# Two ways to place the second batch's turned keys and queries in a fused attention and SwiGLU kernel: by VectorE and by DMA

## The chip, the cores and the metric

The kernel runs on one core of one Trainium2 chip. The metric is the device time of one execution in microseconds; lower is better. The time before is the median of three runs, and a further execution was profiled.

## The reference

Block-sparse attention over q, k, v of shape (4, 8, 768, 64) (batch, heads, sequence, head size), then a gated feed-forward layer over the 3072 tokens with 512 features each.

```python
scores = scale * np.matmul(q, k.transpose(0, 1, 3, 2))      # scale = 1 / sqrt(64)
mask = np.abs(blk_i - blk_j) <= 1                           # blocks of 32 positions
mask = mask | (blk_i == 0) | (blk_j == 0) | (blk_i == 23) | (blk_j == 23)
# and three sampled key blocks for each query block
scores = np.where(mask, scores, -1e9)
attn = softmax(scores)
x = np.matmul(attn, v)                                      # heads side by side: (3072, 512)
xn = x / np.sqrt(np.mean(x * x, axis=-1, keepdims=True) + 1e-06) * rms_g
g = xn @ w_gate                                             # (512, 1536)
out = (g * sigmoid(g) * (xn @ w_val)) @ w_out               # (1536, 512), float32
```

## The kernel before

**Groups and heads.** The work goes in nine groups of rows (called gi). Batch 0 has three groups (gi 0 to 2) of two 128-row tiles; batches 1 to 3 have two groups each (gi 3 to 8) of three tiles. `FIRST` is 3, the first group of batch 1. A group goes through its eight heads in order. For a head, `scores` makes the scores in parts (two in batch 0, three after): PE multiplies `KT` by `QT` into the PSUM tile `st` (L325), and ACT takes the exponential into `ex` (L328). The mask is not a step of its own: 24 more rows of `KT` and `QT` carry it into the product. One head later `late_pv` multiplies `ex` by the values (L336, tile `op`), and DVE divides by the row sums (`rz` L345, `stage` L346).

**The feed-forward pieces.** When a group's attention is done, its rows are scaled (`squares` L370, `rstd` on POOL at L378, `xs`), turned (`tx`, `xg`) and put into a list `fill` of small pieces, which the next group's heads take up one by one at each call of `position()`, four in a head. A gate piece is four matmuls into `gp` (L437) and a tanh on ACT into `th` (L441). A val piece is four matmuls into `vp` (L448) and two DVE instructions: `u` (L452, reads `th` and `gp`) and `hps` (L454, reads `u` and `vp`). A down piece multiplies `hps` by the output weights (`yp` L465); after every fourth of them ACT writes `yo` and SP stores it (L472). `gp`, `vp` and `yp` share three PSUM buffers in turn, so that a `vp` waits until the `u` of the gate before the last has read its `gp`, and a `gp` until a `hps` has read its `vp`.

**Keys and queries of batches 1 to 3.** They come by POOL's DMA queue into `kbf` and `qbf`, a pair of heads at a time (pairs 0 to 3; for batch 1, pairs 0 and 1 early in group 1, pairs 2 and 3 late in group 2). `turn` turns one of them by a DMA transpose on SP's queue (L299) into a `turned` tile, of which there are four buffers in turn. `place` copies the two halves (w = 0 and 1) of a turned tile, 64 partitions of 768 elements each, to partitions 0 to 63 of `KT` or `QT`: for pairs 0 and 1 of batch 1 by DVE (L308), for all others by DMA on SP's queue (L310). Every instruction in a queue waits for those before it: DVE's copies stand among its `u` and `hps`, SP's placings among its turns and stores.

**The order written by hand.** For batch 1 the dictionary `early` says when each step is issued. Its keys count heads from the start of group 2: 0 to 7 are group 2, 8 to 11 the first heads of group 3. A step is a letter and a number: `t` turns, `p` places, and the number is twice the pair, plus 1 for queries. So t0 turns the keys of pair 0 and p3 places the queries of pair 1. All of a head's steps come at its end, in `turns`, after the head's scores, its `late_pv` and its pieces. t4 to t7 use the buffers of t0 to t3 again, so each has to wait until that one is placed. From head 4 of group 3 on, `turns` also turns batch 2 (and later batch 3), a head each, and places the oldest turned tile a head later (`ready`). Heads 2p and 2p + 1 of group 3 are the first that need pair p of batch 1.

Of the kernel before, what the change touches and what calls it, by code (L numbers as in the profile page):

```python
# [18 lines left out]
def kernel(  # L19
# [17 lines left out]
    nc = tc.nc  # L37
    P = 128
    B, H, S, D = q.shape
# [14 lines left out]
    FIRST = NC // 2  # L54
# [39 lines left out]
    def load_qk(b, pr):  # L94
        load_one(b, pr, kbf)
        load_one(b, pr, qbf)

    def load_v(b, pr):
        t = ld.tile([P, 2, NC, D], FP32, name="vraw", tag="vraw" if b else "vraw0",
                    bufs=2 if b else 4)  # L100
        nc.gpsimd.dma_start(  # L101
            out=t, in_=v[b, 2 * pr:2 * pr + 2].rearrange("e (p c) d -> p e c d", p=P))
        vraw[(b, pr)] = t
# [4 lines left out]
    def load_gv(lo, hi):  # L108

        for t, src in ((wg, moe_w_gate), (wv, moe_w_val)):  # L110
            nc.gpsimd.dma_start(
                out=t[:, :, lo * P:hi * P],
                in_=src.rearrange("(c p) f -> p c f", p=P)[:, :, lo * P:hi * P])
# [17 lines left out]
    for h in range(2):  # L131
        for which, src in ((0, k), (1, q)):
# [3 lines left out]
                out=f32[:, 0:cols],  # L136
                in_=src[0, h].rearrange("(p c) d -> p (c d)", p=P)[:, 0:cols])
# [5 lines left out]
    def halves(which, b):  # L143

        if which == 0:
            return KT[b % 2][0:D].rearrange("p h (w c s) -> p h w c s", w=2, s=P)
        return QT[b % 2][0:D].rearrange("p h (c w s) -> p h w c s", w=2, s=P)
# [69 lines left out]
    def mask_keys(lo, hi):  # L217
# [11 lines left out]
                      in_=kind.unsqueeze(1).to_broadcast([NB, H - 4, S]))  # L229
    samp = samp_i[:].rearrange("p (a r w) -> p a r w", r=NRND, w=2)[:, :, :, 0]  # L230
    for r in range(NRND):
        nc.vector.scalar_tensor_tensor(
            out=bm[0:NB, :], in0=samp[0:NB, :, r], scalar=kc[0:NB, :], in1=bm[0:NB, :],
            op0=ALU.is_equal, op1=ALU.max)

    def mask_queries(third):

        c_lo = 2 * third
        cuts = [0] + [(32 * m - c_lo + NC - 1) // NC for m in (1, 2)] + [16]
        for m in range(3):  # L240
            lo, hi = cuts[m], cuts[m + 1]
            nc.vector.tensor_scalar(
                out=qmask.rearrange("p (c i r) -> p c i r", c=NC, r=16)[
                    :, c_lo:c_lo + 2, :, lo:hi],
                in0=bm[0:NB, :].rearrange("p (i m) -> p i m", m=3)[:, :, m].unsqueeze(
                    1).unsqueeze(3).to_broadcast([NB, 2, 8, hi - lo]),
                scalar1=-MASKV, scalar2=MASKV, op0=ALU.mult, op1=ALU.add)

    def spread_queries(third, lo):

        c_lo, c_hi = 2 * third * P, 2 * (third + 1) * P
        nc.sync.dma_start(
            out=QT[0][D:KR, lo:H, c_lo:c_hi],
            in_=qmask[:, c_lo:c_hi].unsqueeze(1).to_broadcast([NB, H - lo, c_hi - c_lo]))
# [38 lines left out]
    turned = {}  # L293
# [9 lines left out]
    def place(b, pr, which):  # L303
        t = turned.pop((b, pr, which))
        view = halves(which, b)[:, 2 * pr:2 * pr + 2]
        for w in range(2):
            if b == 1 and pr < 2:
                nc.vector.tensor_copy(out=view[:, :, w], in_=t[w * D:(w + 1) * D])  # L308
            else:
                nc.sync.dma_start(out=view[:, :, w], in_=t[w * D:(w + 1) * D])  # L310

    def ex_tile(n):
        t = work.tile([P, NC * TGM], BF16, name="ex", tag="ex", bufs=3)
# [2 lines left out]
    def scores(grp, h, part, ex):  # L316

        b, c0, n = grp
        tg = n * P
        nj = 2 if n == HC else 3  # L320
        st = ps_s.tile([P, 1024], FP32, name="st", tag="st")
        at = st.rearrange("p (j t) -> p j t", t=512 if n == HC else tg)
        for e in range(nj):
            jt = nj * part + e
            nc.tensor.matmul(  # L325
                out=at[:, e, 0:tg], lhsT=KT[b % 2][0:KR, h, jt * P:(jt + 1) * P],
                rhs=QT[b % 2][0:KR, h, c0 * P:c0 * P + tg], start=True, stop=True)
        nc.scalar.activation(  # L328
            out=ex[:, nj * part:nj * (part + 1), :], in_=at[:, 0:nj, 0:tg], func=AF.Exp,
            scale=SCALE)  # L330
# [212 lines left out]
    def side_work(gi, h):  # L543

        if gi == 1:
            if h == 0:
                load_gv(3 * NF // 4, NF)
                nc.gpsimd.dma_start(out=wo, in_=moe_w_out.rearrange("(c p) f -> p c f", p=P))
            if h == 1:
                load_qk(1, 0)  # L550
                load_qk(1, 1)
                load_v(1, 0)
                load_v(1, 1)
                held_q.append(qbf[(1, 1)])
            if h == 3:
                mask_queries(2)
                spread_queries(2, 1)
        if gi == FIRST and h == 1:
            nc.gpsimd.dma_start(
                out=gain, in_=moe_rms_g.unsqueeze(0).to_broadcast([P, DM]))  # L560
        if gi == 2 and h == 1:
            for T, m in ((KT, kind), (QT, qmask)):
                nc.gpsimd.dma_start(out=T[1][D:KR, :, :],
                                    in_=m.unsqueeze(1).to_broadcast([NB, H, S]))
        if gi == 2 and h == 2:
            load_one(1, 2, qbf, held_q.pop())
            load_one(1, 2, kbf)
            load_qk(1, 3)
# [9 lines left out]
    def casts(gi, b, g, h):  # L578
# [14 lines left out]
        if b + 1 < B:  # L593
            load_v(b + 1, 2 * g + n)
            load_qk(b + 1, 2 * g + n)

    def turns(gi, b, g, h):


        if gi in (FIRST - 1, FIRST):  # L600
            for step in early.get((gi - FIRST + 1) * H + h, ""):
                pair, which = divmod(int(step[1:]), 2)
                (turn if step[0] == "t" else place)(1, pair, which)
        ready = next(iter(turned), None) if gi > FIRST or (gi == FIRST and h > 3) else None
        if 0 < b < B - 1 and h >= 4:
            turn(b + 1, 2 * g + (h - 4) // 2, h % 2)
        if ready is not None:
            place(*ready)

    early = {0: ("t0", "t1", "t2", "t3"), 5: ("p0",), 6: ("p1", "t4", "t5"),  # L610
             7: ("p2", "t6"), 8: ("p3", "t7", "p4"), 9: ("p5",), 10: ("p6",), 11: ("p7",)}

    TX = 2

# [90 lines left out]
    for gi, grp in enumerate(groups):  # L705
        if gi == 0:
            continue
        b, c0, n = grp
        g = c0 // n
        parts = 3 if n == HC else 2  # L710
        cur = begin(grp)
        for h in range(H):
            ex = ex_tile(n)
            thin = gi == 1 and h < TX
            scores(grp, h, 0, ex)
            if h == 0 and groups[gi - 1][2] == HC:
                squares(waiting[0][0], 2, 0, (H - 1) * D)
            if h == 1 and ending is not None:
                rms_scale(ending, 1)
            if h == TX and ending is not None:  # L720
                transpose_x(ending, 0)
                if gi == 1:
                    transpose_x(ending, 1)
                    enter(ending, NPOS + 4)
                    ending = None
            if thin and h > 0:
                keep_busy(1, 512)
            position()
            if gi == 1 and h == 0:
                late_pv()  # L730
                last = late_pv()
            scores(grp, h, 1, ex)
            side_work(gi, h)
            position()
            if h == TX and ending is not None:
                transpose_x(ending, 2)
            if h == 1 and ending is not None:
                rms_scale(ending, 2)
            if thin:
                keep_busy(1, 512)  # L740
            if gi > 1 or h > 0:
                last = late_pv()
            if last is not None:
                ending = last
            position()
            if parts == 3:
                scores(grp, h, 2, ex)
            position()
            while later:
                later.pop(0)()  # L750
            if h == TX and ending is not None:
                transpose_x(ending, 1)
                enter(ending, NPOS - 2 if gi == len(groups) - 1 else NPOS)
                ending = None
            turn_first(gi, h)
            casts(gi, b, g, h)
            turns(gi, b, g, h)
            if gi == FIRST and h == 5:
                nc.vector.tensor_scalar(out=gain, in0=gain, scalar1=float(DM) ** 0.5,
                                        scalar2=None, op0=ALU.mult)  # L760
            if h == 0 and ending is not None:
                rms_scale(ending, 0)
            if h == H - 1 and n == HC:
                squares(cur, 1, 0, (H - 1) * D)
            waiting.append((cur, h, ex))
# [50 lines left out]
```

## Time and profile before

| | |
|---|---|
| median of 3 runs | 310.85 us (310.80 to 310.89) |
| profiled execution | 311.14 us |
| its span, from the first to the last instruction | 309.4 us |
| PE busy | 298.9 us (97% of the span) |
| DVE busy | 205.9 us (67%) |
| ACT busy | 204.5 us (66%) |
| mean granted TensorE clock | 0.998 |

Times in the views are microseconds from the start of the span; "x4" in a timeline means that four instructions of the same kind were merged into the row, and brackets give the idle time before it and what ended that. PE is TensorE's matmuls, DVE is VectorE, SPq is the queue that issues SyncE's DMAs: a DMA's row there is the time of its issue, and it lands later. Group 2 ends and group 3 begins at about 66 us: its first scores (384 columns wide instead of 256) are the row "66.09 0.49 PE L325 MATMUL st<-QT,KT 88*128 88x384 bf16 x2". With three such rows to a head, head 1 begins at 69.50, head 2 at 73.63, head 4 at 81.68 and head 6 at 89.11.

### The profile page before, as it was taken

The page shows a single profiled execution, that of the slowest core. Times are in us where ns is not written, and L with a number is a line of the kernel's source. Part 1 is how long each engine was busy: PE and PEld are TensorE (multiplying, and loading weights), DVE is VectorE, ACT ScalarE, POOL GpSimd, SP SyncE. Part 2 cuts the span into 40 slices and gives each one's busy share as a digit, 9 for nine tenths or more (in the row PEclk, how much of TensorE's full clock was granted, in tenths as well). Part 3 has the DMA queues.
Part 4 walks back from the last instruction along what each step waited for, and adds up shares of the span by engine and source line. Part 5 has one row for each costly group of instructions (what it writes and reads, how often), then busy time and mean ns, then how long its engine had stood idle before and what let it go on. Part 6 is the DMA issues. An engine that isn't in the chain of part 4 may idle for free.

```text
span 309.4 us, 7249 instructions
## 1 busy us (share of the span) xinstructions
PE 298.9 (97%) x2844; PEld 198.6 (64%) x2864; DVE 205.9 (67%) x568; ACT 204.5 (66%) x330; POOL 55.7 (18%) x81
## 2 busy tenths in 40 slices
PE   7898999999999999999999999999999999999995
PEld 5677886975777566656666566655666566655653
DVE  7888884896668667773768457682767546675850
ACT  4896775775878677657776676676767666733321
POOL 9947120132220212012200122010000100010000
PEclk9999999999999999999999999999999999999999
DMA  7999999899997478506683378714000130002002
GB/s 143 289 205 201 209 245 121 149 189 173 211 170 140 112 155 163 126 20 189 114 157 87 87 170 129 152 30 141 13 2 0 49 106 2 0 18 87 2 0 102
DMA packets 59645, 36.04 MB, mean 117 GB/s; under 512 B 37472, under 2 KB 55204, under 8 KB 59612
## 3 DMA queue, kind: packets, MB, share of 16 engines
q0 software_dynamic: 17120, 17.90, 32.5%
q1 hardware_dynamic: 42456, 17.68, 26.1%
q8 instruction: 22, 0.36, 0.5%
q14 instruction: 11, 0.09, 0.1%
q10 hardware_dynamic: 36, 0.01, 0.1%
HBM read 28.59 MB, written 6.29 MB: 113 GB/s over the span
## 4 chain that ended last, share of the span: by engine, by line
PE 86%; DVE 7%; DMA 2%; issue 1%; SPq 1%; ACT 1%; POOL 0%; DVEq 0%
PE yp L465 20%; PE gp L437 19%; PE vp L448 19%; PE st L325 18%; PE op L336 10%; DMA QT<-turned 2%; SPq L310 1%; DVE junk L370 1%; DVE KT L291 1%; PE tx L419 1%; DVE QT L291 1%; DVE stage L363 1%; DVE hps L454 1%; ACT ex L328 1%; DVE u L452 0%
## 5 line engine op out<-in xcount | busy, mean ns | idle before, releaser
L328 ACT ACTIVATE ex<-st 128x768 bf16<-128x768 f32 x186 | 149.8, 812 | 54.9 <-PE st L325 53.0
L325 PE MATMUL st<-QT,KT 88*128 88x384 bf16 (+1 forms) x432 | 93.8, 308 | 3.4 <-DVE QT L291 1.9
L437 PE MATMUL gp<-xg,wg 128*128 128x384 bf16 (+1 forms) x432 | 80.8, 307 | 0.0
L448 PE MATMUL vp<-xg,wv 128*128 128x384 bf16 (+1 forms) x432 | 80.2, 307 | 0.6 <-DVE u L452 0.6
L452 DVE SCALAR_TENSOR_TENSOR u<-th,gp 128x384 bf16<-128x384 bf16 (+1 forms) x108 | 54.8, 507 | 38.4 <-ACT th L441 36.8
L465 PE MATMUL yp<-wo,hps 128*128 128x512 bf16 (+1 forms) x283 | 71.9, 369 | 0.9
L441 ACT ACTIVATE th<-gp 128x384 bf16<-128x384 f32 (+1 forms) x108 | 48.9, 453 | 27.9 <-PE gp L437 27.7
L454 DVE TENSOR_TENSOR hps<-u,vp 128x384 bf16<-128x384 bf16 (+1 forms) x108 | 55.1, 510 | 11.6 <-DVE u L452 0.5
L325 PEld LDWEIGHTS <-KT 88*128 88x128 bf16 x432 | 41.2, 98 | 28.5 <-DVE QT L291 2.8
L448 PEld LDWEIGHTS <-wv 128*128 128x128 bf16 x432 | 40.6, 97 | 21.5 <-issue 1.0
L437 PEld LDWEIGHTS <-wg 128*128 128x128 bf16 x432 | 40.1, 97 | 20.5 <-issue 0.3
L336 PEld LDWEIGHTS <-ex 128*128 128x128 bf16 x1116 | 42.8, 97 | 8.6 <-issue 0.2
L336 PE MATMUL op<-Vp,ex 128*128 128x66 bf16 x1116 | 44.9, 193 | 0.0
L465 PEld LDWEIGHTS <-hps 128*128 128x128 bf16 x300 | 27.7, 97 | 22.3
L378 POOL TENSOR_TENSOR rstd<-ssq,mhalf 128x3 f32<-128x3 f32 (+1 forms) x9 | 7.3, 815 | 148.3 <-DVE ssq L370 148.3
L345 DVE RECIPROCAL rz<-op 128x3 f32<-128x3 f32 (+1 forms) x64 | 11.2, 174 | 23.5 <-PE op L336 23.2
L471 ACT ACTIVATE yo<-yp 128x512 f32<-128x512 f32 (+1 forms) x25 | 14.4, 576 | 15.5 <-PE yp L465 15.5
L346 DVE TENSOR_TENSOR stage<-op,rz 128x192 bf16<-128x192 f32 (+1 forms) x64 | 21.8, 341 | 2.2
L101 POOL DMA_DIRECT2D vraw<-in_v_dram x16 | 12.0, 753 | 57.3 <-DVE Vp L120 50.5
L370 DVE CUSTOM_DVE_ANT_0 junk<-stage 128x448 bf16<-128x448 bf16 (+1 forms) x24 | 14.7, 611 | 0.5
L390 DVE SCALAR_TENSOR_TENSOR xs<-stage,rstd,gain 128x512 bf16<-128x512 bf16 x15 | 10.4, 748 | 4.4 <-POOL rstd L378 4.4
L89 POOL DMA_DIRECT2D qbf<-in_q_dram x12 | 8.7, 728 | 14.9 <-DMA turned<-qbf 14.1
(72 smaller groups left out, 115.5 us busy)
## 6 DMA issues: line engine op xcount, KB each, us to landing
vraw<-in_v_dram POOLq DMA_DIRECT2D x16, 384.0 KB, 5.1
out_dram<-yo SPq DMA_DIRECT2D x23, 256.0 KB, 2.2
kbf<-in_k_dram POOLq DMA_DIRECT2D x15, 192.0 KB, 5.5
qbf<-in_q_dram POOLq DMA_DIRECT2D x12, 192.0 KB, 6.1
KT<-turned SPq DMA_DIRECT2D x20, 96.0 KB, 4.3
QT<-turned SPq DMA_DIRECT2D x20, 96.0 KB, 2.4
wg<-in_moe_w_gate_dram POOLq DMA_DIRECT2D x4, 384.0 KB, 9.0
wv<-in_moe_w_val_dram POOLq DMA_DIRECT2D x4, 384.0 KB, 11.0
```

The costliest lines, as they stand in the source:

```text
L325: nc.tensor.matmul(out=at[:, e, 0:tg], lhsT=KT[b % 2][0:KR, h, jt * P:(jt + 1) * P], rhs=QT[b % 2][0:KR, h, c0 * P:c0 * P + tg], start=Tru ...
L328: nc.scalar.activation(out=ex[:, nj * part:nj * (part + 1), :], in_=at[:, 0:nj, 0:tg], func=AF.Exp, scale=SCALE)
L336: nc.tensor.matmul(out=op[:, it, 0:VW], lhsT=ex[:, jt, it * P:(it + 1) * P], rhs=Vp[b % 2][:, h, 2 * (jt % HC) + jt // HC, 0:VW], start=(j ...
L346: nc.vector.tensor_tensor(out=stage[:, 0:n, h * D:(h + 1) * D], in0=op[:, 0:n, 0:D], in1=rz[:, 0:n].unsqueeze(2).to_broadcast([P, n, D]), ...
L370: nc.vector.tensor_tensor_reduce(out=junk[:, 0:hi - lo], in0=part, in1=part, scale=1.0, scalar=(e["ssq"][:, it:it + 1] if lo else DM * 1e- ...
L437: nc.tensor.matmul(out=gp[:, 0:tg], lhsT=wg[:, c, f * P:(f + 1) * P], rhs=xg[:, c, 0:tg], start=(c == 0), stop=(c == KD - 1))
L441: nc.scalar.activation(out=th[:, 0:tg], in_=gp[:, 0:tg], func=AF.Tanh, scale=0.5)
L448: nc.tensor.matmul(out=vp[:, 0:tg], lhsT=wv[:, c, f * P:(f + 1) * P], rhs=xg[:, c, 0:tg], start=(c == 0), stop=(c == KD - 1))
L452: nc.vector.scalar_tensor_tensor(out=u[:, 0:tg], in0=th[:, 0:tg], scalar=1.0, in1=gp[:, 0:tg], op0=ALU.add, op1=ALU.mult)
L454: nc.vector.tensor_tensor(out=hps[:, f, 0:tg], in0=u[:, 0:tg], in1=vp[:, 0:tg], op=ALU.mult)
L465: nc.tensor.matmul(out=yp, lhsT=hps[:, f, tt * P:(tt + 1) * P], rhs=wo[:, f, lo:hi], start=(f == 0), stop=(f == NF - 1))
L471: nc.scalar.mul(out=yo, in_=yp, mul=0.5)
```

## The change

`place` always uses DMA. A new function `place_half` copies one half of a turned tile by DVE, and only pair 0 of batch 1 uses it: its four half copies are steps `w` (`w10` is half 0 of step number 1, the queries of pair 0). Keys of `early` get a second number: 0 for the new place in the middle of a head, after its second part of scores (`batch_one(gi, h, 0)`), 1 for the end of the head as before. Pair 1 (p2 and p3) is placed by DMA at the end of head 6, ahead of t4 and t5; t6 and t7 are issued at the end of head 7; p4 and p5 at the end of head 8, p6 and p7 at the end of head 9. The generic placing may begin at head 2 of group 3 instead of head 4.

```diff
@@ place @@
         for w in range(2):
-            if b == 1 and pr < 2:
-                nc.vector.tensor_copy(out=view[:, :, w], in_=t[w * D:(w + 1) * D])
-            else:
-                nc.sync.dma_start(out=view[:, :, w], in_=t[w * D:(w + 1) * D])
+            nc.sync.dma_start(out=view[:, :, w], in_=t[w * D:(w + 1) * D])
+
+    def place_half(b, pr, which, w):
+        t = turned[(b, pr, which)]
+        view = halves(which, b)[:, 2 * pr:2 * pr + 2]
+        nc.vector.tensor_copy(out=view[:, :, w], in_=t[w * D:(w + 1) * D])
+        if w:
+            del turned[(b, pr, which)]
...
+    def batch_one(gi, h, at):
+        for step in early.get(((gi - FIRST + 1) * H + h, at), ""):
+            pair, which = divmod(int(step[1]), 2)
+            if step[0] == "w":
+                place_half(1, pair, which, int(step[2]))
+            else:
+                (turn if step[0] == "t" else place)(1, pair, which)
+
     def turns(gi, b, g, h):
         if gi in (FIRST - 1, FIRST):
-            for step in early.get((gi - FIRST + 1) * H + h, ""):
-                pair, which = divmod(int(step[1:]), 2)
-                (turn if step[0] == "t" else place)(1, pair, which)
-        ready = next(iter(turned), None) if gi > FIRST or (gi == FIRST and h > 3) else None
+            batch_one(gi, h, 1)
+        ready = next(iter(turned), None) if gi > FIRST or (gi == FIRST and h > 1) else None
...
-    early = {0: ("t0", "t1", "t2", "t3"), 5: ("p0",), 6: ("p1", "t4", "t5"),
-             7: ("p2", "t6"), 8: ("p3", "t7", "p4"), 9: ("p5",), 10: ("p6",), 11: ("p7",)}
+    early = {(0, 1): ("t0", "t1", "t2", "t3"), (5, 0): ("w00",), (5, 1): ("w01",),
+             (6, 0): ("w10",), (6, 1): ("p2", "p3", "t4", "t5"), (7, 0): ("w11",),
+             (7, 1): ("t6", "t7"), (8, 1): ("p4", "p5"), (9, 1): ("p6", "p7")}
...
             scores(grp, h, 1, ex)
+            if gi in (FIRST - 1, FIRST):
+                batch_one(gi, h, 0)
             side_work(gi, h)
```

## The prediction

> **What bounds the kernel now.** I read the page first, then the waits in the stretch where the edit lies, then the timelines of PE, DVE and SP there. The page's first rows:
>
> ```profile
> span 309.4 us, 7249 instructions
> PE 298.9 (97%) x2844; PEld 198.6 (64%) x2864; DVE 205.9 (67%) x568; ACT 204.5 (66%) x330; POOL 55.7 (18%) x81
> ```
>
> PE is busy 298.9 of 309.4 us, so only a wait of PE can be won or lost. The waits between 55 and 100 us name just two that stop PE itself (columns: us in total, times, longest):
>
> ```profile
> PE st L325 <- DMA QT<-turned: 0.7, 1, 0.7
> PE vp L448 <- DVE u L452: 0.6, 2, 0.4
> ```
>
> The same view from 100 to 296 us has no row of PE, so what is won before 100 us should reach the end, and so should what is lost. PE's timeline shows where they are:
>
> ```profile
> 61.77 0.60 PE L437 MATMUL gp<-xg,wg 128*128 128x256 bf16 x4
> 62.31 0.60 PE L448 MATMUL vp<-xg,wv 128*128 128x256 bf16 x4
> ...
> 64.65 0.60 PE L437 MATMUL gp<-xg,wg 128*128 128x256 bf16 x4
> 65.66 0.60 PE L448 MATMUL vp<-xg,wv 128*128 128x256 bf16 x4 [0.41 <-DVE u L452]
> ...
> 68.42 0.49 PE L325 MATMUL st<-QT,KT 88*128 88x384 bf16 x2
> 69.07 0.60 PE L448 MATMUL vp<-xg,wv 128*128 128x256 bf16 x4 [0.15 <-DVE u L452]
> ...
> 87.81 0.60 PE L448 MATMUL vp<-xg,wv 128*128 128x256 bf16 x4
> 89.11 0.49 PE L325 MATMUL st<-QT,KT 88*128 88x384 bf16 x2 [0.70 <-DMA QT<-turned]
> ```
>
> Starts tell the size better than modelled ends. Undisturbed, a gp is followed after 0.44 us, an st after 0.33, a vp after 0.43. The four distances here are 0.54, 1.01, 0.65 and 1.30, so the waits are 0.10, 0.57, 0.32 and 0.87: together 1.86 us, the most that this edit can win.
>
> The first three belong to DVE, which works from 58.1 to 72.8 us without a break:
>
> ```profile
> 60.90 0.90 DVE L308 COPY KT<-turned 64x768 bf16<-64x768 bf16 x2
> ...
> 64.44 0.71 DVE L308 COPY QT<-turned 64x768 bf16<-64x768 bf16 x2
> 65.18 0.42 DVE L452 SCALAR_TENSOR_TENSOR u<-th,gp 128x256 bf16<-128x256 bf16 x1
> ...
> 67.85 0.72 DVE L308 COPY KT<-turned 64x768 bf16<-64x768 bf16 x2
> 68.59 0.42 DVE L452 SCALAR_TENSOR_TENSOR u<-th,gp 128x256 bf16<-128x256 bf16 x1
> ```
>
> Each late vp starts just after a u ends (65.60 and 65.66, 69.01 and 69.07), and ahead of that u stand copies of L308. The fourth wait is head 6 of group 3, which needs pair 3. SP's queue shows why that comes late:
>
> ```profile
> 68.59 1.21 SPq L299 DMA_TRANSPOSE turned<-kbf  x1
> 72.45 1.21 SPq L299 DMA_TRANSPOSE turned<-qbf  x1
> 73.72 1.38 SPq L310 DMA_DIRECT2D KT<-turned  x2
> ...
> 78.85 0.34 SPq L472 DMA_DIRECT2D out_dram<-yo  x1
> 79.23 1.25 SPq L310 DMA_DIRECT2D KT<-turned  x2
> 80.52 3.19 SPq L310 DMA_DIRECT2D QT<-turned  x2
> ```
>
> The last turn (t7, 72.45) waits for the buffer that DVE empties in its copy from 71.45 to 72.43, and p7 (80.52) is issued into the loads that POOL issues from 79.77 on; its DMAs take 6.6 and 8.2 us to land. The last lands at 88.98, PE starts at 89.11.
>
> **DVE's copies.** Eight half copies become four: w00 before the first u of head 5, w01 and w10 side by side where p0 stood, w11 where p1 stood; p2's and p3's copies go. A half copy lasts 346 ns in the median row (345 to 616), and with its gap holds the queue 0.36; p0 held it 0.94, p1 0.74, p2 0.74. I follow the four u's.
> - w00: the u at 58.74 starts when its th is ready (58.33 + 0.38), so w00 is paid in full: the u ends at 59.52 where the vp at 59.43 reuses its buffer. A new wait, +0.14.
> - w01 and w10: 0.72 for 0.94, behind a lag of 0.36: the u of 61.84 goes to 61.98, its vp from 62.31 to 62.45 (+0.14 in all).
> - w11: 0.36 for 0.74: the u of 65.18 goes to 64.94, its vp from 65.66 to 65.42 (PE arrives at 65.23): 0.24 ahead of before.
> - p2 gone: the u of 68.59 goes to 67.61 and ends at 68.03, before PE arrives at 68.51. The 0.32 goes too: 0.56 ahead.
> So 0.56 is won. Bounds: all copies at 0.62 instead of 0.36 give +0.93 at 62.31, +0.81 at 65.66 and +0.49 in the end, a loss; no cost anywhere gives the full 0.99. I take 0.56, because six of the eight copies took 345 to 356 ns. p3's removed copies (0.98 from 71.45) delayed no PE work; xs (L398) behind them simply comes earlier. What is late next in this stretch is ACT, whose th follows each gp by some 0.9 us, and PE's order already allows for that.
>
> **p2 and p3 on SP.** Four DMA issues of 0.6 us (row L310: median 600 and 617 ns) are 2.4 us. SP's timeline shows nothing from 53.88 to 65.44, where t4 waits for the load of kbf. p2 needs t2, p3 needs t3, both landed at 60.3 by the trace, so I put the issues at 59.8 to 62.3. Queued behind are t4 to t7, and until kbf is in they wait anyway: nothing on SP. On the DMA engines the 384 KB meet a gap: between 60 and 66 us (slices of 0.15 us) the engines stand nearly idle from 61.05 to 62.4 and are full from 63 on:
>
> ```profile
> DMA  9999999000000003970299999999999999899969
> ```
>
> At the 200 to 400 GB/s of that window 384 KB are 1 to 2 us. Unfinished, they push kbf, qbf and vraw back by 0 to 2 us. Pair 1 is first read by head 2 of group 3 at 73.63: over 8 us of cover, and the placing DMAs before take 2.3 to 8.2. If that cover were gone, PE would wait one for one.
>
> **The turns.** t5 now waits for w11 (64.94), t6 for p2, t7 for p3, instead of for copies that ended at 65.15, 68.57 and 72.43. With the 2 us above t4 starts at 67.4 at the latest and t7, three steps of 1.35 later, at 71.4, so 1.0 us or more before 72.45. p4 and p5 follow directly (four issues, to about 75.3), then the yo, then p6 and p7 to 78.4 instead of 83.7, before the yo of 78.85 and before POOL's loads of 79.77. Even with the worst landing, 8.2, pair 3 is there at 86.6; head 6 would arrive at 88.24 - 0.56 = 87.68. The 0.87 goes; bounds 0 and 0.87. Pair 2 needs head 4 at 81.68 - 0.56 = 81.12, and p5, issued by 75.3 with the 4.5 us that placings of this moment took, is there by 79.8.
> The generic placing, now allowed from head 2 instead of head 4 of group 3, finds nothing turned there: nothing.
>
> **Sum.** 0.56 + 0.87 = 1.43. The profiled execution took 311.14 (span 309.4 and 1.74 around it), so 309.71 for it; the median of the runs is 310.85, 0.29 lower, so 309.42, said as 309.4. Less than 0.2% (0.62 us) is about what a measurement of this kernel cannot tell from no change.
>
> **Rivals.**
> - *The copies collide with POOL.* POOL issues loads from 60.91 to 64.50, and w01 and w10 fall into it. Two copies of before, both during POOL's issues, took 542 and 616 ns; two others there took 346. With these two at 0.62, the vp's go to +0.66, +0.28 and -0.04: DVE wins nothing, 0.91 is left, 309.95. The Trainium skill, SBUF — State Buffer, section Who interferes with whom, says that a copy in a two-port mode and a GpSimd instruction exclude each other for a whole instruction. The trace agrees in part: 616 ns is far from 346 plus POOL's 0.73. By the rule a blocked copy would be an estimated 1.08, and the two would cost almost 0.9 more at 62.31. Chance 0.16, of which 0.03 within 0.2%.
> - *Head 6 waits as before*, because SP or the loads hold p7 back after all: 310.85 - 0.56 = 310.3, within 0.2%. For it speaks that p6's second half took 6.6 from 79.87; against it that p7 goes out 4 us sooner. Chance 0.09.
> - *Pair 1 comes late and holds the turns: slower.* A transfer on SP's queue could need the 14.0 us that t1 took (45.30 to 59.28). p3's second half from 61.7 then lands at 75.7, t7 starts at 75.8, 3.35 later than before, p5 lands not at 80.26 but at 83.6, and head 4, due at 81.12, waits 2.5: -1.43 + 2.5 = +1.1, or 311.9. It decides when p3 lands after 75.2. Against it: t1 stood behind the mask copies, which landed at 58.97 and 59.51, and nothing like them runs here. For it: p3 moves rows of 128 bf16, 256 bytes each. The Trainium skill, DMA: Bandwidth & Descriptors, section Specifications, puts the smallest piece for line rate at 512 B. The trace does not show that: QT's placings, in such pieces, have a median of 2.4 us and KT's, in longer ones, 4.3. Chance 0.11, of which 0.09 slower by over 0.2%.
> - *All of the 1.86 goes*: 309.0. It needs w00 to be free. Chance 0.06.
>
> **The numbers.** My forecast, both wins, has 0.58. Faster by over 0.2%: 0.58 + 0.06 + 0.13 = 0.77. Same: 0.03 + 0.09 + 0.02 = 0.14. Slower: 0.09. The range goes from 309.0 (everything won) to 310.4: the low bound of the copies with the 0.87 won is 310.85 - 0.87 + 0.49 = 310.47, and the second rival lies just inside. It leaves out the slow rival and some edge of the others, together under 0.2.
>
> **What would show it.** In the changed profile: four copies of 64x768 at the new line, near 58.7, 61.3, 61.6 and 64.6; a new small distance before the vp at 59.4; the vp's near 65.4 and 68.5 with at most 0.2 us of wait in front; t7 issued before 72 and p7 before 79; no wait of st on QT<-turned; PE's later work some 1.4 us earlier. I would be wrong if DVE's copies last 0.5 us or more, if an st of heads 2 to 4 in group 3 waits for a DMA, or if a wait of PE appears after 100 us.

## The result, and the profile after

| | before | changed |
|---|---|---|
| median, 12 runs each, side by side | 310.82 us (310.11 to 311.45) | 310.05 us (309.41 to 310.47) |
| ratio | | 0.9973 (0.9962 to 0.9984) |
| profiled execution, its span | 311.14, 309.4 us | 310.47, 308.7 us |

The change is faster by 0.27% by the ratio, some 0.84 us (0.50 to 1.18); the medians are 0.77 apart. A second comparison of the same kernel gave 0.9976 (0.9965 to 0.9988). The forecast was 309.4, a win of 1.43; the direction and the range held, the size is little over half. The first rows of the changed kernel's page (DVE has four instructions fewer):

```profile
span 308.7 us, 7250 instructions
## 1 busy us (share of the span) xinstructions
PE 299.6 (97%) x2844; PEld 199.2 (65%) x2864; DVE 205.2 (66%) x564; ACT 204.4 (66%) x330; POOL 54.7 (18%) x81
```

The waits between 55 and 100 us hold one row that stops PE, where there were two:

```profile
PE vp L452 <- DVE u L456: 0.2, 1, 0.2
```

PE's timeline at the places shown before (this execution was already 0.62 us later at head 1 of group 2, in work that the diff doesn't touch, so compare distances and not positions):

```profile
59.61 0.60 PE L441 MATMUL gp<-xg,wg 128*128 128x256 bf16 x4
60.42 0.60 PE L452 MATMUL vp<-xg,wv 128*128 128x256 bf16 x4 [0.21 <-DVE u L456]
...
62.76 0.60 PE L441 MATMUL gp<-xg,wg 128*128 128x256 bf16 x4
63.30 0.60 PE L452 MATMUL vp<-xg,wv 128*128 128x256 bf16 x4
...
65.64 0.60 PE L441 MATMUL gp<-xg,wg 128*128 128x256 bf16 x4
66.39 0.60 PE L452 MATMUL vp<-xg,wv 128*128 128x256 bf16 x4
...
69.16 0.49 PE L329 MATMUL st<-QT,KT 88*128 88x384 bf16 x2
69.48 0.60 PE L452 MATMUL vp<-xg,wv 128*128 128x256 bf16 x4
...
88.22 0.60 PE L452 MATMUL vp<-xg,wv 128*128 128x256 bf16 x4
88.66 0.49 PE L329 MATMUL st<-QT,KT 88*128 88x384 bf16 x2
```

The distances are 0.81, 0.54, 0.75, 0.32 and 0.44: waits of 0.37 (new), 0.11, 0.31, none, none. From the second part of scores of head 1 in group 2 (45.34, before 44.72) to the first of head 1 in group 4 (98.57, before 99.02) it took 53.23 us instead of 54.30, 1.07 less; this is called the stretch below. DVE's rows around its copies:

```profile
58.76 0.77 DVE L120 CAST Vp<-vraw 128x768 bf16<-128x768 f32 x1
59.46 0.59 DVE L312 COPY KT<-turned 64x768 bf16<-64x768 bf16 x1
59.97 0.40 DVE L456 SCALAR_TENSOR_TENSOR u<-th,gp 128x256 bf16<-128x256 bf16 x1
...
65.43 0.08 DVE L374 DVE_READ_ACCUMULATOR2_ANT ssq<- 128x1 f32 x1
65.53 0.35 DVE L312 COPY QT<-turned 64x768 bf16<-64x768 bf16 x1
65.91 0.42 DVE L456 SCALAR_TENSOR_TENSOR u<-th,gp 128x256 bf16<-128x256 bf16 x1
```

w00 lasted 0.59 and the cast ahead of it 0.77 (0.55 in before), both while POOL issued loads:

```profile
58.42 1.45 POOL L89 DMA_DIRECT2D kbf<-in_k_dram  x2
59.84 0.73 POOL L89 DMA_DIRECT2D qbf<-in_q_dram  x1
```

w11 took the queue from 65.43 to 65.91, 0.48 where 0.36 was reckoned. SP's rows are as forecast in this profile, even earlier: t7 at 68.62 (72.45 before), p7's two halves at 76.64 (80.52):

```profile
65.86 1.21 SPq L299 DMA_TRANSPOSE turned<-qbf  x1
67.18 1.34 SPq L299 DMA_TRANSPOSE turned<-kbf  x1
68.62 2.39 SPq L299 DMA_TRANSPOSE turned<-qbf  x1
...
75.32 1.27 SPq L307 DMA_DIRECT2D KT<-turned  x2
76.64 1.29 SPq L307 DMA_DIRECT2D QT<-turned  x2
```

### The profile page after: what moved, and what is told of

Read it like the earlier page. It is cut to its first block, busy times and chain, and to the rows that moved or that the text cites. A ratio compares the mean times of both kernels' runs of the same rounds, so it can differ in the third digit from the quotient of the medians.

```text
span 308.7 us, 7250 instructions
## 1 busy us (share of the span) xinstructions
PE 299.6 (97%) x2844; PEld 199.2 (65%) x2864; DVE 205.2 (66%) x564; ACT 204.4 (66%) x330; POOL 54.7 (18%) x81
## 4 chain that ended last, share of the span: by engine, by line
PE 91%; DVE 6%; issue 1%; ACT 1%; POOL 0%; DVEq 0%
PE yp L469 20%; PE gp L441 20%; PE vp L452 20%; PE st L329 19%; PE op L340 10%; PE unread L170 1%; DVE junk L374 1%; PE tx L423 1%; DVE KT L291 1%; DVE QT L291 1%; DVE u L456 1%; DVE stage L367 1%; DVE hps L458 1%; ACT ex L332 1%; PE tfirst L153 0%
## 5 line engine op out<-in xcount | busy, mean ns | idle before, releaser
L89 POOL DMA_DIRECT2D kbf<-in_k_dram x15 | 11.0, 734 | 0.8 <-issue 0.8
```

## The experiments

Two theories at the start. A: splitting pair 0's copies wins nothing, because w00 meets POOL's issues and a half from partitions 64 to 127 costs more than one from 0 to 63; the win is pair 1's copies gone and the sooner turns. B: the forecast's sizes hold and the first profile was unlucky. The edits change the table of steps.

**Whole copies at the old places.**

```diff
-  (5, 0): w00   (5, 1): w01   (6, 0): w10   (6, 1): p2 p3 t4 t5   (7, 0): w11
+  (5, 1): w00 w01             (6, 1): w10 w11 p2 p3 t4 t5
```

> The changed kernel with pair 0's keys copied as two adjacent halves at the end of head 5 and its queries at the end of head 6 (the places of before); everything else as changed. Theory A: in the changed kernel the splitting wins nothing, because the first half (w00) falls on POOL's load issues and a half that reads partitions 64 to 127 (w = 1) holds DVE's queue for some 0.48 us wherever it stands. Then here the waits of vp are those of before at the first two places (0.10 and 0.57), the third (0.32) is gone, head 6's 0.87 too: 1.19 us less than before, the same as the changed kernel within 0.2 us. Rival B (the forecast's sizes hold and the profiled execution was only unlucky): the changed kernel is the faster by 0.24 us.

The ratio to before is 0.9984 (0.9972 to 0.9997), so the interval overlaps that of the changed kernel (0.9973), which leaves a small win of splitting open. In the one profile of this kernel the only wait in the stretch is 0.49 at the vp of 66.2, in place of the changed kernel's 0.79. B's 0.24 in favour of splitting is not seen there.

**Splitting alone, in the kernel before.**

```diff
-  (5): p0   (6): p1 t4 t5   (7): p2 t6   (8): p3 t7 p4             # p0 to p3 by DVE
+  (5, 0): w00   (5, 1): w01   (6, 0): w10   (6, 1): t4 t5
+  (7, 0): w11   (7, 1): w20 w21 t6   (8, 1): w30 w31 t7 p4
```

> The kernel before with one part of the change: pair 0 in four half copies at the changed places. Pair 1 stays with DVE at the ends of heads 7 and 8, the turns and placings stay at the heads of before (t5 behind w11). Theory A (splitting wins nothing, the gain comes from pair 1's copies gone and from the sooner turns): the wait at the vp of 62.3 grows, the one of 65.7 shrinks by about as much, the one of 69.1 (0.32) and head 6's (up to 0.87) stay; the same time as before within 0.2%. Rival B (the forecast's sizes of the halves): 0.24 us less at the vp of 65.7.

Ratio 1.0003 (0.9994 to 1.0013). The waits of vp are 0.59, 0.31 and 0.32: what the third place won (0.57 to 0.31) the second lost, and more (0.11 to 0.59), where w01 and w10 met POOL's issues and lasted 0.61 and 0.67. A holds. Head 6 did not wait at all here, though p7 went out at 80.82: a first doubt about the 0.87.

**Pair 1 by DMA, without the sooner order.**

```diff
-  (5): p0   (6): p1 t4 t5   (7): p2 t6   (8): p3 t7 p4             # p0 to p3 by DVE
+  (5, 1): w00 w01   (6, 1): w10 w11 t4 t5   (7, 1): p2 t6   (8, 1): p3 t7 p4   # p2, p3 by DMA
```

> The kernel before with another part alone: pair 1 is placed by DMA, at the heads of before (p2 at the end of head 7, p3 of head 8, ahead of t7); pair 0 by adjacent half copies at the places of before; turns and placings at the heads of before. Theory A: the third vp wait (0.32) goes; t7 follows p3's issue and no longer a copy that ends at 72.4, so it starts by 71, and head 6's wait goes too, since late placing alone did not bring it back: about 1.1 us less than before in the stretch. Rival B (all of the sooner order is needed): only 0.32 is won, head 6 waits 0.5 to 0.9.

Both were wrong: 317.15 us, ratio 1.0216 (1.0195 to 1.0236), 6.5 us slower. SP's rows and PE's first wait:

```profile
66.40 1.52 SPq L307 DMA_DIRECT2D KT<-turned  x2
71.99 1.24 SPq L299 DMA_TRANSPOSE turned<-kbf  x1
73.28 1.32 SPq L307 DMA_DIRECT2D QT<-turned  x2
77.33 1.23 SPq L299 DMA_TRANSPOSE turned<-qbf  x1
```

```profile
77.34 0.80 PE L329 MATMUL st<-QT,KT 88*128 88x384 bf16 x2 [3.99 <-DMA QT<-turned]
```

p2 now stands behind t4 and t5. t6 must wait until p2 has landed (t6 starts 5.6 us after p2's issue), p3 stands behind t6 and lands just ahead of 77.33, when both t7 and PE's head 2 go on. This is the slow rival of the prediction in kind, but by another chain: PE waits for p3 itself at head 2, where the rival had head 4 waiting for p5. The wait, 4.15 us by starts, is not the whole price. The granted clock is 0.50 in every window from 77 to 83 us and 1.00 up to 75 and from 84 on, and a row of two st matmuls that takes 0.49 elsewhere takes 0.84 at 79.64. At half clock from 77.3 to 83.3 PE loses an estimated 3.0 us; with the wait that is 7.1, by which this stretch (59.98 us) is longer than the one with whole copies (52.92). What excludes the wait in the change is the order: p2 and p3 go out ahead of t4 (56.57 to 59.91, t4 at 62.50).

**All of batch 1 by DMA.**

```diff
-  (5, 0): w00   (5, 1): w01   (6, 0): w10   (6, 1): p2 p3 t4 t5   (7, 0): w11
+  (5, 1): p0 p1                             (6, 1): p2 p3 t4 t5
```

> Pair 0 is placed by DMA too (p0 and p1 at the end of head 5), everything else as changed: DVE copies nothing. Theory A: all waits of vp between 57 and 70 us go (0.99 in before, 0.78 in the changed kernel) and head 6's 0.87 stays gone: 1.8 us less than before, about 0.8 less than the changed kernel, if the queries' halves land before head 0 of group 3 (66 us). Rival B: p1 lands late because the turn t1 can take 14 us; then the first st of group 3 waits, by up to some 3 us, and the kernel is slower than before.

Every wait of vp is gone, and no st waits. The place that had waits of 0.57 and 0.31 stands at its undisturbed distance of 0.44:

```profile
64.59 0.60 PE L441 MATMUL gp<-xg,wg 128*128 128x256 bf16 x4
65.03 0.60 PE L452 MATMUL vp<-xg,wv 128*128 128x256 bf16 x4
```

The stretch took 52.44 us, 1.86 less than in the first profile of before and 0.79 less than in the changed kernel's. So A is right on where PE waited. Yet the time is 309.81 us, ratio 0.9978 (0.9964 to 0.9991), no better than the changed kernel. Most of the difference is at the other end: from the start of the last matmul to the end of the span this kernel takes 4.22 us, before 3.77, the changed kernel 3.55 (the last section tells why, as far as it is known).

**The keys' halves a head sooner.**

```diff
-  (5, 0): w00   (5, 1): w01
+  (4, 0): w00   (4, 1): w01
```

> As changed, but the keys' two half copies stand a head sooner (w00 in the middle of head 4, w01 at its end), where DVE waits for ACT (idle 0.92 and 0.58 us there in before) and where POOL does not yet issue loads; w10 and w11 stay. Theory A (what w00 cost was lag that it added just ahead of a u, and POOL's collision): the distances before the vp's of 59.4, 62.3 and 65.7 fall to 0.44 to 0.5, so about 0.6 to 0.8 us less than the changed kernel and 1.6 to 1.8 less than before. Rival B (the lag comes from DVE's load as a whole, wherever the copies stand): the same waits as in the changed kernel, the same time within 0.2 us.

Ratio 0.9974 (0.9961 to 0.9987), the same as the changed kernel. w01 now stood where w00 had stood, right behind the cast; it met POOL's issues there (0.53, with the cast ahead of it at 0.76), and the vp waits are 0.52 and 0.13. So the edit did not free that place of a copy, the expected 0.6 was not won, and A and B are not told apart by it. Whether a copy there meets the issues differs from execution to execution: POOL's first issue stood between 57.0 and 61.2 us in these profiles, because it waits for t3 to land.

**The placings of pairs 2 and 3 as late as before.**

```diff
-  (8, 1): p4 p5   (9, 1): p6 p7          # generic placing from head 2
+  (8, 1): p4   (9, 1): p5   (10, 1): p6   (11, 1): p7   # generic placing from head 4
```

> As changed up to the turns, but p4 to p7 are issued as late as in the kernel before (one a head, at the ends of heads 0 to 3 of group 3, and the generic placing from head 4). It tells apart what removed head 6's wait of 0.87. Theory A (the wait was the late placing: p7 goes out after the yo of 78.9 and into POOL's loads, whenever its turn was ready): the wait is back, 0.5 to 0.9 us, and the kernel is slower than the changed one by that. Rival B (the sooner turn t7 alone did it): p7 lands sooner all the same, no wait of st, the same time as the changed kernel.

In the profile head 6 doesn't wait, although p7 was issued at 80.31 as in before. Its second half was issued by 80.97 instead of 82.37. The time is 310.22 us, ratio 0.9987 (0.9973 to 1.0001), which leans to the slow side of the changed kernel, with overlapping intervals. So the wait need not come back with late placings. But the second profile of before, next, has none either with p7 at 80.43 and 82.26, so this run does not show that the sooner turn removed it.

**Both kernels once more, for a second profile.**

> The changed kernel once more, for a second profile. If w00's cost in the first one was chance (its copy met POOL's load issue), the distances before the vp's of some 59 and 66 us differ by 0.1 to 0.3 from the first profile's (0.81 and 0.75), with copies of 0.35 instead of 0.59; if the cost is in the order itself, they repeat within 0.05.

> The kernel before once more, for a second profile and to see what a comparison of a kernel with itself gives (a ratio of 1.000, within 0.15%). Theory: the three vp waits (0.10, 0.57, 0.32) repeat within 0.2 in sum. Open is head 6's wait: if it hangs on chance in the DMA queues it is not the same 0.87 here.

The second comparison of the changed kernel gave 0.9976, that of before with itself 1.0005 (0.9993 to 1.0017). In the changed kernel's second profile w00 lasted 0.34 and there is no wait at the first place; the others are 0.22 and 0.31. So w00's cost was chance, the 0.31 is not. The 0.22 is the collision again, on another copy: w10 lasted 0.56 while POOL issued loads from 61.18 on. Nor is the sooner turn there in every execution: t3 landed later, and t7 went out at 72.34, as late as in before and later than the 71.4 that the prediction gave as its latest; p7 still went out at 78.37, ahead of POOL's loads of 79.33. In before's second profile the vp waits are 0.55 and 0.32 again, but head 6 goes on at once:

```profile
87.70 0.60 PE L448 MATMUL vp<-xg,wv 128*128 128x256 bf16 x4
88.14 0.49 PE L325 MATMUL st<-QT,KT 88*128 88x384 bf16 x2
```

Instead gp waits 20 us later for the turned rows of the next feed-forward pieces, which SP issues behind the placings of batch 2, and the same wait stands in the second profile of the changed kernel. First before, then changed:

```profile
107.53 0.65 PE L437 MATMUL gp<-xg,wg 128*128 128x384 bf16 x3 [0.52 <-DMA xg<-xs]
```

```profile
107.50 0.81 PE L441 MATMUL gp<-xg,wg 128*128 128x384 bf16 x4 [0.82 <-DMA xg<-xs]
```

By starts these are 0.68 and 0.99. Neither first profile has it. For head 6 the two profiles of before differ in the landing: p7's first half, issued at 80.52 and 80.43, took 8.2 and 6.7 us, and the three loads that POOL issued beside it took 1.5 to 1.8 us longer in the first as well.

**The halves exchanged.**

```diff
-  (5, 0): w00   (5, 1): w01   (6, 0): w10   (7, 0): w11
+  (5, 0): w01   (5, 1): w00   (6, 0): w11   (7, 0): w10
```

> The changed kernel with the two halves of each tile exchanged: the halves from partitions 64 to 127 (w = 1) are copied at the middles of heads 5 and 6, the halves from partitions 0 to 63 at the end of head 5 and the middle of head 7. In the traces so far a w = 0 half holds DVE's queue some 0.28 us and a w = 1 half 0.48 when each stands alone, because the instruction ahead of it and the one behind it do not overlap with it. If that is so, the lag before the vp near 65.7 is smaller by 0.2 than in the changed kernel (0.31 there becomes 0.1 to 0.15) and the one near 59.4 larger (some 0.15 to 0.3 where POOL does not interfere). Rival: each half costs the same 0.36, and the distances stay as they were within 0.05.

The wait at the third place is 0.08 (0.31, 0.31, 0.30 and 0.31 in four profiles with w11 there), the first 0.16, the second 0.20. DVE's rows at the third place:

```profile
65.41 0.08 DVE L374 DVE_READ_ACCUMULATOR2_ANT ssq<- 128x1 f32 x1
65.41 0.35 DVE L312 COPY QT<-turned 64x768 bf16<-64x768 bf16 x1
65.68 0.40 DVE L456 SCALAR_TENSOR_TENSOR u<-th,gp 128x256 bf16<-128x256 bf16 x1
```

The copy from partitions 0 to 63 starts with the accumulator's read and u starts before the copy ends: 0.27 of the queue, against w11's 0.48 with the same duration of 0.35. The theory of the halves holds. The sum of the three waits is 0.44, within the spread of the changed kernel's, and the time the same: ratio 0.9974 (0.9963 to 0.9986). This profile, too, has the wait of gp for xg, 0.89 by starts at 108.01.

**The turns of xg ahead of the placing at head 0**, in three kernels: all by DMA, changed, and before.

```diff
             turn_first(gi, h)
             casts(gi, b, g, h)
+            if h == 0 and ending is not None:
+                rms_scale(ending, 0)
             turns(gi, b, g, h)
...
-            if h == 0 and ending is not None:
-                rms_scale(ending, 0)
```

`rms_scale` also makes `xs` on DVE, so in the kernel before the exchange is not on SP alone: at head 0 of group 3 the copies of p3 now stand behind the first xs (71.72 instead of 71.45).

> All of batch 1 placed by DMA (as in the earlier run), and at head 0 of a group the turns of xs into xg are issued ahead of that head's placing for the next batch, whose own turn SP otherwise waits for. Theory (with the copies gone and the wait of gp on xg gone, nothing of the stretch is left): no wait of vp, st or gp between 55 and 110 us, about 1.5 us less than before on average and 0.7 less than the changed kernel. Rival: the placing, now behind the xg turns, or the turns of xg themselves wait elsewhere, and the time is that of the all-DMA kernel or more.

> The changed kernel with that exchange on SP alone. Theory: the wait of gp on xg<-xs near 107 us, which came in the second profile of the changed kernel (0.99) and of the kernel before (0.68) but not in the first ones, is gone in every execution; its median falls by 0.2 to 0.6 us against the changed kernel's. Rival: the wait is rare or moves to another transfer, and the time stays within 0.2 us of the changed kernel's.

> The kernel before with the same exchange on SP alone. Theory: in the kernel before either head 6 of group 3 waits (0.87) or, where it does not, gp waits for xg (0.68), since the first makes PE late for the second; so taking the second away wins as much as in the changed kernel or more, and leaves the waits of vp (0.9 to 1.0) and now and then head 6's. Rival: xg is no wait in most executions, and the time is that of before within 0.2 us.

All three were slower: 311.59, 311.98 and 312.84 us, ratios 1.0037 (1.0023 to 1.0050), 1.0050 (1.0024 to 1.0076) and 1.0077 (1.0049 to 1.0106). The wait did not go; most of it moved to later groups (near 142, 179 and 215 us), and in the all-DMA kernel one of the three is still at 106 us. From 100 to 296 us the all-DMA kernel and the changed one with the exchange have (neither first profile has a row of PE there):

```profile
PE gp L441 <- DMA xg<-xs: 1.1, 3, 0.6
```

```profile
PE gp L441 <- DMA xg<-xs: 1.4, 2, 1.2
```

In the changed kernel's case SP issues the first turn at 171.23, then a placing, and the others only at 174.95 and 176.91, where without the exchange all three were out by 177.05 with no placing between (171.93, 173.93, 175.83). The placing was not removed; it now stands between the turns. These three profiles are each of the fastest run of their kernel (311.54, 311.49 and 311.39), so they show less than the medians lost, and what the slower runs lost was not seen. The guess about the order was wrong, and the version that was to beat both kernels does not. In the profiles of before and of the changed kernel with the exchange, the waits of vp were 0.49 and 0.32, and 0.05 and 0.31, and head 6 did not wait: two more observations for the sums below.

## Why the prediction was right or wrong

All waits of PE in the stretch, by starts (0 is under 0.05); the rows with the exchange (xg first) serve too, since it touches nothing up to 70 us, and at head 6 in before it makes t7 later (72.70), not sooner:

| profile | first (59.4) | second (62.3) | third (65.7) | fourth (69.1) | sum of vp | head 6 |
|---|---|---|---|---|---|---|
| forecast for the changed kernel | 0.14 | 0.10 | 0.19 | 0 | 0.43 | 0 |
| before | 0 | 0.11 | 0.57 | 0.32 | 1.00 | 0.87 |
| before, second | 0 | 0 | 0.55 | 0.32 | 0.87 | 0 |
| before, xg first | 0 | 0 | 0.49 | 0.32 | 0.81 | 0 |
| changed | 0.37 | 0.11 | 0.31 | 0 | 0.79 | 0 |
| changed, second | 0 | 0.22 | 0.31 | 0 | 0.53 | 0 |
| changed, xg first | 0 | 0.05 | 0.31 | 0 | 0.36 | 0 |
| changed, placings late | 0 | 0.06 | 0.30 | 0 | 0.36 | 0 |

**The bound** was right: PE's waits make the difference, and DVE's copies and SP's order make those waits. With no copy on DVE at all they vanish.

**DVE's term, 0.56, was mis-sized.** The means of the sums are 0.89 and 0.51, so 0.38 was won. The fourth place came out exactly: with p2's copies gone its 0.32 goes in every profile. The step that failed is w11 at "0.36 for 0.74": it is 0.48 for 0.74, hence 0.31 at the third place and not 0.19, four times out of four. To reckon each half alike, at 0.36, was the error; the two halves are 0.27 and some 0.48. w00 "paid in full" was too much in three of four profiles, where the vp behind it came in time (in the second it put its u off by 0.16, from 58.74 to 58.90), and too little in the first one, where it and the cast ahead of it met POOL's issues. So the first rival, the collision, does happen, in two of the four profiles: on w00 in the first (0.37) and on w10, where the prediction had looked for it, in the second (0.22).

A win by splitting was not seen. Whole copies left 0.49 in one profile, split ones 0.36 to 0.79, and splitting alone changed nothing. The copies of pair 1 that went to the DMA are the win on DVE.

**Head 6's term, 0.87, was a wait of one execution.** The step that failed was to read it, from one profile, as something that every execution pays, with the bounds 0 and 0.87 and the upper end taken. It is in one of three profiles of before, and in none of the kernel with splitting alone, whose SP order is that of before. A mean of about 0.2 to 0.3 is all that these few profiles support. The mechanism, p7 issued into POOL's loads by a full queue, is consistent with its rows, and with the sooner placings it was not seen again; what the DMA queues do differently from one execution to the next was not isolated.

**What was won and given back:** a PE that is not held at head 6 can be held at gp near 107 us for xg (0.68 in before, 0.99 in the changed kernel). "No row of PE from 100 to 296 us" was true of that profile and not of the kernel. A wait after 100 us was one of the prediction's three signs of being wrong, and a copy of 0.5 us or more another; both came, each in some executions, while the third, an st of heads 2 to 4 that waits, did not.

**The sum, remade:** 0.38 for DVE and 0.22 at the tail (below), 0.60 in all, are seen in the profiles. The fastest runs, 310.11 and 309.41 in both comparisons, are 0.70 apart. The measured 0.84 and 0.75 leave 0.15 to 0.24 for head 6 less the waits of xg. So small a remainder is argued and not shown, with intervals of 0.3 to either side. No term of the prediction names the tail; without its 0.22 the win would be 0.62, so that the size came as near as it did is in part luck.

The sum leaves out one more difference: from 11 us on PE is 0.4 to 0.7 us later than in before in five of the profiles (changed, late placings, whole copies, keys sooner, halves exchanged) and within 0.1 in all others, two of the changed kernel among them. The diff touches no instruction there; whether it is chance was not tested.

**The rivals.** All of the 1.86 going was seen with everything on DMA, for the stretch alone. The slow rival was not the change but a smaller edit, pair 1 by DMA without the new order: it is one step away and costs 6.5 us, almost half of it, by the estimate above, through the lower clock behind the wait, which the rival's price of 2.5 for the wait alone left out. I had set its deciding point by p3's landing alone; the point is what stands ahead of p2 and p3 on SP.

## What to carry to other kernels

A wait on a transfer in one profile is one draw: profile the kernel a second time before a term of a sum is made of it, and ask where PE would be held next if it were gone. Work that moves from an engine to a DMA queue needs its place in that queue more than a low price: issued well ahead of the turns that reuse its source, the same move won; issued so late that these turns stood until it had landed, it lost 2%. A pair of adjacent copies is not two equal halves; take the pitch from the start of the instruction before to the start of the one behind, for each half on its own.

## What the runs showed of the hardware that was not expected

**Copies from the upper partitions hold the queue.** A copy reading partitions 64 to 127 held DVE for 0.48 us, one reading 0 to 63 for 0.27, both lasting 0.35. The former starts only when its predecessor has ended (65.43 + 0.08, then 65.53), and its successor only when it has ended (65.53 + 0.35, then 65.91). The Trainium skill, VectorE: DVE Perf Modes, section Two Vector instructions with no wait between them, says that an instruction whose input starts in another group of 32 partitions than that of the last one to read the same memory is held until all earlier ones have finished. The rows agree, and 0.21 us is its price here.

**A copy that meets POOL's issues** lasted 0.53 to 0.67 instead of 0.35 (once 0.43) and the cast of 0.55 up to 0.80; in other executions copies under the same issues lasted 0.36. In three profiles it went the other way: the cast kept its 0.55, and the POOL issue under way beside it lasted 0.80 to 0.87 where the others near it take 0.71 to 0.76. The prediction's estimate of 1.08 for a blocked copy was not seen.

**The tail depends on the number of DMAs on SP.** From the issue of the last store to the end of the span it is 3.06 us in before and 2.83 in the changed kernel. The waits on SP from 304 us on, before and then changed:

```profile
SPq L811 <- DMA out_dram<-yo: 1.3, 1, 1.3
```

```profile
SPq L825 <- DMA out_dram<-yo: 1.0, 1, 1.0
```

At the end SP waits for its eight DMA semaphores in a fixed order, some 0.065 us each. In before the last store is on the first of them, so that the others are waited for after it has landed; with four more DMAs on SP it is on the fifth, and the first four have been dealt with while it is under way. From the start of the last matmul to the end it was 3.77, 3.77, 3.78 and 3.77 in four profiles with before's number of DMAs and 3.53 to 3.56 in seven with four more (3.68 in an eighth, the one with late placings of pair 1). With eight more, all by DMA, the store is on the first again, and the tail was 4.22 twice; the further 0.45 was not explained (0.33 of it stands ahead of the last of the eight waits, in both profiles).
